# A gated linear recurrence with a SiLU feed-forward block on one core: a block of short products of several tile shapes behind the last product

## The chip, the cores and the metric

The kernel runs on one core of one Trainium2 chip. The metric is the device time of one execution in microseconds (us); of several executions the median is given. A profile of one execution lies beside the times. Its engines are called by the names of the profile: PE is TensorE's matmul, PEld its weight load, DVE VectorE, ACT ScalarE, POOL GpSimd and SP SyncE; a name with a q behind it (PEldq, SPq) is that engine's instruction queue, where waits, branches and transfers are issued.

## What is computed

Two blocks follow each other. The first is a recurrence over 768 steps for 4 batches of 8 heads with 48 x 48 complex states; the second takes its output as 3072 tokens of 384 numbers through a feed-forward block with 2048 hidden units.

```python
for t in range(S):                                   # S = 768, per batch and head, D = 48
    S_re, S_im = a_re*S_re - a_im*S_im + outer(k[t], v[t]),  a_re*S_im + a_im*S_re
    y[t] = q[t] @ S_re                               # a normalised to a magnitude of at most 0.999
x = y.transpose(0, 2, 1, 3).reshape(3072, 384)
h = x @ w_in                                         # 384 x 2048
out = (h * sigmoid(h)) @ w_out                       # 2048 x 384
```

## The kernel before

The 3072 tokens are cut into 24 chunks of 128 steps (`n`), two chunks make a pair (`p`, 12 of them). For each chunk the recurrence becomes products of 128 x 128 weights with the running state of 96 rows (48 real, 48 imaginary): `state` and `state_of_pairs` (lines 695 to 719) sum keys and values into the new state, `weights` (line 607) makes the scores, `output` (line 629) the result. For each pair the feed-forward block runs in eight steps `jp`: `hidden` makes two times 128 hidden units in one PSUM bank of the tag `h` (two banks that take turns, pool `p_h`, line 138), `silu` evicts it on ACT, and `result` adds its product with the second weight matrix into four (or two) accumulators `o`.

From pair 2 on the products of the feed-forward block are done in three parts of a shorter float type (`fp32r`), so that the sum has nearly the precision of float32. One set of parts, the rounded second weight matrix `W["coarse"]` (line 900, 128 rows x 16 x 384), stays in SBUF until the end. It is written by ACT (line 904) in the first third of the span and only read from then on.

The products of the recurrence are plain float32. On PE each of them is two records of weights and two of products, as the counts show: line 705 stands for 6 chunks x 8 heads, that is 48 products, and has 96 records. A `fp32r` product is one record.

The shapes matter below. Line 705 multiplies weights of 128 rows x 96 columns with 48 moving columns and uses the whole array. Lines 645, 648 and 716 write to `ps[64 * r:64 * r + 64]` with r = 0 and 1 in turn, so each uses one half of the array's columns. No product of the kernel before uses 64 rows, half of the array's rows, alone.

The order of all work is written out by hand in one long string of steps (lines 1129 to 1271), which is issued under `manual_schedule`; each engine gets its instructions in that order. Its last steps are `r:11.7` (the last twelve products, line 1004), then `oc:11.0` and `oc:11.1` (line 1014), which evict the last two accumulators, each in two halves, one on DVE (line 1021) and one on ACT (line 1023), and store them (line 1034). Behind the string every engine reads the flag `weak` (`values_load`, line 1279) and branches on it (line 1280) past a slower second program that is not taken here. Then the program closes: SP waits for one semaphore after the other, and all engines meet (the lines 1280 and 1442 of the profile).

Of the kernel before, what the change touches and what calls it, by code (L numbers as in the profile page):

```python
# [11 lines left out]
F32 = mybir.dt.float32  # L12
# [58 lines left out]
def kernel(  # L71
# [19 lines left out]
    nc = tc.nc  # L91
    B, H, S, D = q.shape
    C = 128
# [4 lines left out]
    D2 = 2 * D  # L98
# [4 lines left out]
    T = 2 * C  # L103
# [34 lines left out]
    p_h = Ring(fast.enter_context(tc.tile_pool(name="p_h", bufs=1, space=PSUM)), 2)  # L138
# [307 lines left out]
    def upper(n, x):  # L446

        p, i = divmod(n, 2)
        t = X[n][x] = room("left").tile([C, 2, DM], F32R, tag="part", name=f"{x}_parts{n}", bufs=1)
        nc.scalar.copy(out=t[:, 0], in_=cut(A[p][x], i))  # L450

    def lower(n, x):

        p, i = divmod(n, 2)
        t = X[n][x]
        nc.vector.tensor_tensor(out=t[:, 1], in0=cut(A[p][x], i), in1=t[:, 0].bitcast(F32),
                                op=ALU.subtract)
# [74 lines left out]
    def decayed(n, which="kq"):  # L532
        x = X[n]
        for w in which:
            e, at = x["e" + w], x[w].rearrange("p h d -> p (h d)")
            to = at if n < STRAIGHT else e
            if w == "k" and n >= STRAIGHT:
                nc.vector.scalar_tensor_tensor(out=to, in0=e, scalar=MOST, in1=at, op0=ALU.min,
                                               op1=ALU.mult)
            else:  # L540
                nc.vector.tensor_tensor(out=to, in0=at, in1=e, op=ALU.mult)
            x["e" + w] = to
            x[w, "decayed"] = True

    def rotated(n, which="kq", hs=slice(None)):

        x = X[n]
        for w in which:
            e = x["e" + w]
            if w + "r" not in x:  # L550
                spare = w == "k" and n in (1, 3)
                if spare:
                    x[w + "r"] = spare_form("xH", n // 2, f"{w}r{n}").rearrange(
                        "p (h c d) -> p h c d", h=H, c=2)
                else:
                    x[w + "r"] = att.tile([C, H, 2, D], F32, tag=w + "r", name=f"{w}r{n}", bufs=1)
            to, cs = x[w + "r"][:, hs], x["cs"][:, hs]
            nc.vector.tensor_tensor(
                out=to, in0=heads(e)[:, hs].unsqueeze(2).to_broadcast(list(to.shape)), in1=cs,
                op=ALU.mult)  # L560
# [26 lines left out]
    def squared(n, i):  # L587
        x = X[n]
        if "sq" not in x:
            x["sq"] = room("left").tile([C, NB, 2, HH, 2 * Q], F32, tag="sq", name=f"sq{n}", bufs=1)  # L590
        to = x["sq"][:, :, i].rearrange("p b h (j r) -> p b h r j" if i == 0 else
                                        "p b h (r j) -> p b h r j", r=2)
        of = x["kq"[i] + "r"].rearrange("p h c d -> p h (c d)")
        nc.vector.transpose(to, of.rearrange("p (h r) (b j) -> p b h r j", r=2, j=Q))
# [225 lines left out]
    V = {}  # L820
# [75 lines left out]
    W = {}  # L896
# [139 lines left out]
    def warm(n):  # L1036
# [3 lines left out]
        for _ in range(n):  # L1040
            nc.tensor.matmul(ps[:, 0], lhsT=any_[:, 0:C], rhs=any_, start=True, stop=True)

    def half_of(n, w, i):
        rotated(n, w, slice(i * HH, (i + 1) * HH))

# [50 lines left out]
    for name, f in {  # L1096
            "e0": early_square, "e1": early_magnitude, "e2": early_log, "e3": early_half,
            "e4": early_excess, "e5": early_l, "e6": early_add, "e7": early_inverse,
            "e8": early_ratio, "exp": decays, "phase": phases, "rd": rounded, "turn": turn,
            "trig": trig,  # L1100
            "ends": ends_of, "thirds": thirds, "L": summed, "carried": carried,
            "last": last_of, "dk": lambda n: decayed(n, "k"),
            "dq": lambda n: decayed(n, "q"), "K": lambda n: rotated(n, "k"),
            "Q": lambda n: rotated(n, "q"), "tk": lambda n: squared(n, 0),
            "tq": lambda n: squared(n, 1), "td": homed, "s": state, "ss": state_squared,
            "sd": state_homed, "S": carried_on, "y": output, "x": put, "xd": third_of,
            "ht": lambda n: upper(n, "th"), "hl": lambda n: upper(n, "l"),
            "ut": lambda n: lower(n, "th"), "ul": lambda n: lower(n, "l"),
            "xh": x_head, "xt": x_tail, "xg": x_diff,
            "vh": v_head, "vt": v_tail, "vk": v_kept, "vl": v_home,  # L1110
            "G0": squares, "G1": gates_log, "G2": gates_excess, "G3": gates_inverse,
            "G4": gates_l, "G5": magnitude, "G6": gates_ratio, "G7": gates_add,
            "G8": gates_side, "G9": gates_atan, "Ga": gates_angle, "of": finish,
            "wq": w_rounded, "wd": w_tail, "ws": w_diff, "wk": w_kept,
            "sm": small, "lk": looked_at, "ck0": check_decays, "ck1": check_low, "ck2": check_fit,
            "ck3": check_gathered, "ck4": check_weak,
    }.items():
        early[name] = lambda x, f=f: f(int(x))
    for name, f in {
            "rk": lambda n, i: half_of(n, "k", i), "rq": lambda n, i: half_of(n, "q", i),  # L1120
            "t": turned, "T": placed, "w": weights, "m": masked, "h": hidden, "g": silu,
            "lv": v_loaded, "vx": v_mixed, "oc": copied,
            "r": result, "gr": g_rounded, "gb": g_tail, "gc": g_diff,
            "lw": w_loaded, "at": lambda p, i: gates_atan(p, i),
            "an": lambda p, i: gates_angle(p, i),
    }.items():
        early[name] = lambda x, f=f: f(*map(int, x.split(".")))
    with tc.manual_schedule():
        for x in """
# [137 lines left out]
                r:11.4 lw:10.6 h:11.7 gc:11.5 lk:30 r:11.5 g:10.6 gr:10.6 h:10.7 gb:10.6 gc:10.6  # L1267
                lw:10.7 g:11.7 gb:11.6 lk:29 gc:11.6 r:10.6 gr:11.7 g:10.7 gr:10.7 ck2:0 gb:11.7
                gb:10.7 gc:10.7 ck3:0 r:10.7 ck4:0 oc:10.0 r:11.6 gc:11.7 oc:10.1 r:11.7 oc:11.0
                oc:11.1  # L1270
                """.split():
            what, _, arg = x.partition(":")
            early[what](arg)
# [173 lines left out]
```

## Time and profile before

| | |
|---|---|
| median of 2 executions | 606.19 us (605.37 to 607.02) |
| profiled execution, span from its first to its last instruction | 603.4 us |
| what lies around the span, by the median | 2.8 us (2.0 to 3.6 by the two executions) |
| PE, PEld busy | 583.3 us (97%), 509.3 us (84%) |
| DVE, ACT, POOL busy | 495.7 us (82%), 441.2 us (73%), 222.5 us (37%) |
| granted TensorE clock, mean of the span | 0.984 |

The profile gives no time of its own for the profiled execution besides its span; the median stands 2.8 us above it. A row of the timeline gives a start and a length in us from the first instruction, then engine, line, operation, output<-inputs with weights x moving operand, and a count. A record's length is longer than the time to the next record's start, because products are pipelined: where the price of a product is wanted, starts are compared. The granted clock is 1.00 at the higher of TensorE's two levels (2.4 GHz) and 0.50 at the lower (1.2 GHz).

### The profile page before, as it was taken

The page shows a single profiled execution, that of the slowest core. Times are in us where ns is not written, and L with a number is a line of the kernel's source. Part 1 is how long each engine was busy: PE and PEld are TensorE (multiplying, and loading weights), DVE is VectorE, ACT ScalarE, POOL GpSimd, SP SyncE. Part 2 cuts the span into 40 slices and gives each one's busy share as a digit, 9 for nine tenths or more (in the row PEclk, how much of TensorE's full clock was granted, in tenths as well). Part 3 has the DMA queues.
Part 4 walks back from the last instruction along what each step waited for, and adds up shares of the span by engine and source line. Part 5 has one row for each costly group of instructions (what it writes and reads, how often), then busy time and mean ns, then how long its engine had stood idle before and what let it go on. Part 6 is the DMA issues. An engine that isn't in the chain of part 4 may idle for free. (4 is left out here: it accounts for less than half of the span.)

```text
span 603.4 us, 11507 instructions
## 1 busy us (share of the span) xinstructions
PE 583.3 (97%) x3828; PEld 509.3 (84%) x3828; DVE 495.7 (82%) x765; ACT 441.2 (73%) x695; POOL 222.5 (37%) x389
## 2 busy tenths in 40 slices
PE   8588999999999999999999999999999999999997
PEld 6367877787767998998898898998898898999996
DVE  5899999987998989989889888889878786654644
ACT  7999999889885698896898895897884552342332
POOL 6364543636231534554444441536720323000000
PEclk9589999999999999999999999999999999999999
DMA  8988688977869977777868777859768467445652
GB/s 177 253 186 197 181 195 185 224 195 174 224 206 265 216 187 185 161 152 209 193 162 210 162 158 204 174 147 211 151 169 245 141 183 205 147 155 172 210 184 83
DMA packets 167728, 112.23 MB, mean 186 GB/s; under 512 B 137724, under 2 KB 143424, under 8 KB 167664
## 3 DMA queue, kind: packets, MB, share of 16 engines
q1 hardware_dynamic: 151920, 89.69, 57.2%
q0 software_dynamic: 12288, 17.23, 14.4%
q10 hardware_dynamic: 3456, 4.52, 2.1%
q8 instruction: 32, 0.52, 0.4%
q14 instruction: 32, 0.26, 0.2%
HBM read 81.14 MB, written 11.47 MB: 153 GB/s over the span
## 5 line engine op out<-in xcount | busy, mean ns | idle before, releaser
L307 ACT ACT_TABLE_LOAD x69 | 88.5, 1283 | 2.3 <-ACT ot L1017 0.8
L313 ACT ACTIVATE g<-h 128x512 f32<-128x512 f32 x96 | 56.0, 593 | 46.0 <-PE h L783 23.9
L600 POOL DMA_DIRECT2D T<-sq x120 | 70.1, 609 | 31.1 <-PE a L613 10.6
L944 ACT ACTIVATE head<-g 128x512 fp32r<-128x512 f32 x75 | 47.2, 630 | 46.2 <-PE o L986 25.9
L888 DVE SCALAR_TENSOR_TENSOR tail<-g,head 128x512 fp32r<-128x512 f32 x75 | 51.3, 683 | 32.1 <-ACT head L944 16.7
L528 POOL DMA_DIRECT2D dec<-ends x48 | 32.7, 722 | 117.6 <-DMA ends<-eq 116.8
L986 PE MATMUL o<-coarse,head 128*128 128x384 f32 x256 | 57.1, 344 | 0.5 <-ACT ot L1017 0.5
L766 PE MATMUL h<-xL,fine 128*128 128x512 f32 x192 | 55.3, 396 | 0.4 <-DMA fine<-w_firsts 0.4
L766 PE MATMUL h<-xD,mixed 128*128 128x512 f32 x192 | 55.2, 396 | 0.4 <-DVE xD L892 0.3
L986 PE MATMUL o<-diff,gd 128*128 128x384 f32 x256 | 55.4, 337 | 0.0
L892 DVE TENSOR_TENSOR gd<-tail,g 128x512 fp32r<-128x512 f32 x75 | 51.5, 687 | 4.3
L734 POOL DMA_DIRECT2D S<-ssq x84 | 46.8, 601 | 16.2 <-DVE ssq L723 10.3
L613 PEld LDWEIGHTS a<-T 96*128 96x128 f32 x384 | 49.9, 196 | 2.6 <-ACT T L605 0.3
L613 PE MATMUL a<-T 96*128 96x128 f32 x384 | 51.7, 281 | 0.1
L986 PEld LDWEIGHTS o<-coarse,head 128*128 128x128 f32 x256 | 44.8, 188 | 4.1 <-issue 1.1
L986 PE MATMUL o<-fine,tail 128*128 128x384 f32 x224 | 48.0, 336 | 0.0
L986 PEld LDWEIGHTS o<-diff,gd 128*128 128x128 f32 x256 | 45.5, 188 | 0.2 <-DVE gd L892 0.2
L776 PE MATMUL h<-xT,w 128*128 128x256 f32 x192 | 43.7, 381 | 1.6 <-ACT xT L689 1.6
L766 PEld LDWEIGHTS h<-xD,mixed 128*128 128x128 f32 x192 | 35.7, 188 | 10.1 <-DVE xD L892 1.2
L766 PEld LDWEIGHTS h<-xL,fine 128*128 128x128 f32 x192 | 36.0, 188 | 9.4 <-DMA fine<-w_firsts 0.8
L968 PE MATMUL o<-w,g 128*128 128x384 f32 x128 | 43.5, 488 | 0.0
L776 PEld LDWEIGHTS h<-xT,w 128*128 128x128 f32 x192 | 36.0, 190 | 7.9 <-ACT xT L689 1.8
(182 smaller groups left out, 1400.1 us busy)
## 6 DMA issues: line engine op xcount, KB each, us to landing
fine<-w_firsts SPq DMA_DIRECT2D x40, 384.0 KB
diff<-w_diffs SPq DMA_DIRECT2D x40, 384.0 KB
T<-sq SPq DMA_DIRECT2D x120, 64.0 KB
T<-sq POOLq DMA_DIRECT2D x120, 64.0 KB, 3.6
small<-in_moe_w_in_dram SPq DMA_DIRECT2D x16, 384.0 KB
raw<-in_moe_w_out_dram SPq DMA_DIRECT2D x16, 384.0 KB
small<-in_moe_w_out_dram SPq DMA_DIRECT2D x16, 384.0 KB
raw<-in_moe_w_in_dram SPq DMA_DIRECT2D x24, 192.0 KB
```

The lines of the kernel that those rows point to most:

```text
L307: nc.scalar.preload_act_table_set(SETS[of][0])
L313: nc.scalar.activation(out=out, in_=in_, func=func, **kw)
L600: (nc.gpsimd if a % 2 else nc.sync).dma_start(out=to[ts(b, Q), :, a], in_=X[n]["sq"][ts(a, Q), b].rearrange("p w h x -> p (w h) x"))
L613: nc.tensor.matmul(ps[:, h], lhsT=x["kT"][hh * HH + h], rhs=x["qT"][hh * HH + h], start=True, stop=True)
L734: (nc.gpsimd if g % 2 else nc.sync).dma_start(out=to[ts(b, Q), r, :, e], in_=sq[ts(g, Q), :, b, 0:e.stop - e.start])
L766: nc.tensor.matmul(ps, lhsT=w[:, dc, ts(p % 2, C)], rhs=x[:, :, dc], start=(f == 0 and dc == 0), stop=(f == len(forms) - 1 and dc == ND - 1))
L776: nc.tensor.matmul(ps[:, ji], lhsT=of_first(w1, dc, jp * 2 + ji), rhs=A[p]["xT"][:, dc], start=(dc == 0), stop=(dc == ND - 1))
L888: nc.vector.scalar_tensor_tensor(out=dst, in0=whole, scalar=MORE / FINER, in1=head.bitcast(F32), op0=ALU.mult, op1=ALU.subtract)
L892: nc.vector.tensor_tensor(out=dst, in0=tail, in1=whole, op=ALU.subtract)
L944: nc.scalar.mul(g_form(p, jp, "head"), A[p]["g", jp], MORE * SPLIT / FINER)
L968: nc.tensor.matmul(A[p]["o"][m].rearrange("p n c -> p (n c)"), lhsT=A[p]["g", jp][:, ji, ts(m, C)], rhs=w2[jp][:, ji], start=(j == 0), sto ...
L986: nc.tensor.matmul(A[q_]["o"][m].rearrange("p n c -> p (n c)"), lhsT=left[:, i, ts(m, C)], rhs=right, start=(first_ and n == 0), stop=(las ...
```

## The change

A step `after` is added, and put behind the last step of the order. It issues 100 products on PE, all from `W["coarse"]`, into tiles of the two banks of the tag `h`, which no one reads. `plain` is the same memory called float32, so 88 of the 100 are float32 products (two records each) and the 12 with 384 moving columns are `fp32r` (one record). In order: three groups of 16 with 64 rows, upper and lower half of the rows in turn, into two banks (96, 128 and 96 weight columns, 48, 48 and 64 moving columns); 8 over all rows, 96 x 48; 8 with 64 rows, 128 x 384; 8 with 96 rows and 64 columns, the halves of the columns in turn; 16 with 64 rows and 64 columns, the four quarters of the array in turn; 8 with 64 rows, 96 x 48; 4 over all rows, 128 x 384. Nothing else changes; the output is the same.

```diff
+    def after(_):
+        of = W["coarse"].rearrange("p j n -> p (j n)")
+        plain = of.bitcast(F32)
+        other = V["coarse", 4]
+
+        def bank():
+            return p_h.tile([C, 2, T], F32, tag="h", name="after").rearrange("p i x -> p (i x)")
...
+        for wide, narrow in ((D2, D), (C, D), (D2, 64)):
+            two = [bank(), bank()]
+            for i in range(8):
+                for s in range(2):
+                    at = slice(64 * s, 64 * s + 64)
+                    nc.tensor.matmul(two[s][0:wide, ds(narrow * (i % 8), narrow)],
+                                     lhsT=plain[at, ds(128 * i, wide)],
+                                     rhs=plain[at, ds(2048 + 64 * i, narrow)], start=True, stop=True)
+        one = bank()
+        for i in range(8):
+            nc.tensor.matmul(one[0:D2, ts(i, D)], lhsT=plain[:, ds(128 * i, D2)],
+                             rhs=plain[:, ds(2048 + 64 * i, D)], start=True, stop=True)
+        two = [bank(), bank()]
+        for i in range(4):
+            for s in range(2):
+                at = slice(64 * s, 64 * s + 64)
+                nc.tensor.matmul(two[s][:, 0:384], lhsT=of[at, ts(i, C)],
+                                 rhs=of[at, 2048:2432], start=(i == 0), stop=(i == 3))
+        two = [bank(), bank()]
+        for i in range(4):
+            for r in range(2):
+                nc.tensor.matmul(two[0][64 * r:64 * r + 64, ts(i, 64)], lhsT=plain[0:D2, ts(r, 64)],
+                                 rhs=plain[0:D2, 0:64], start=True, stop=True)
+        for i in range(4):
+            for s in range(2):
+                for r in range(2):
+                    at = slice(64 * s, 64 * s + 64)
+                    nc.tensor.matmul(two[s][64 * r:64 * r + 64, ds(256 + 64 * i, 64)],
+                                     lhsT=plain[at, ts(2 * i + r, 64)],
+                                     rhs=plain[at, ds(2048 + 64 * i, 64)], start=True, stop=True)
+        two = [bank(), bank()]
+        for i in range(4):
+            for s in range(2):
+                at = slice(64 * s, 64 * s + 64)
+                nc.tensor.matmul(two[s][0:D2, ts(i, D)], lhsT=plain[at, ds(128 * i, D2)],
+                                 rhs=plain[at, ds(2048 + 64 * i, D)], start=True, stop=True)
+        ps = bank()
+        for i in range(4):
+            nc.tensor.matmul(ps[:, 0:384], lhsT=of[:, ts(i, C)], rhs=of[:, 2048:2432],
+                             start=(i == 0), stop=(i == 3))
...
-                oc:11.1
+                oc:11.1 after:0
```

On PE, at the end of the program of before, the flag's load and the branch follow the last product of pair 11 (`o_1` is its second accumulator):

```order
L1004 MATMUL o_1_6293<-coarse,forms_7_6748 128x384 x2
L1004 MATMUL o_1_6293<-fine_1828,forms_7_6748 128x384 x2
L1004 MATMUL o_1_6293<-diff_7_6729,forms_7_6748 128x384 x2
L1279 TENSOR_LOAD weak [waits DVE_49]
L1280 COMPARE_AND_BRANCH
```

The same place now. Here 96x48 is the output of one product (weight columns x moving columns), x16 a count, and PE_49 the semaphore that PE itself raises, so such a wait is PE's for its own earlier product in that bank:

```order
L1004 MATMUL o_1_6293<-diff_7_6729,forms_7_6748 128x384 x2
L1061 MATMUL after<-coarse 96x48 [waits PE_49] x2
L1061 MATMUL after<-coarse 96x48 x14
L1061 MATMUL after<-coarse 128x48 [waits PE_49] x2
L1061 MATMUL after<-coarse 128x48 x14
L1061 MATMUL after<-coarse 96x64 [waits PE_49] x2
L1061 MATMUL after<-coarse 96x64 x14
L1066 MATMUL after<-coarse 96x48 [waits PE_49]
L1066 MATMUL after<-coarse 96x48 x7
L1072 MATMUL after<-coarse 128x384 [waits PE_49] x2
L1072 MATMUL after<-coarse 128x384 x6
L1077 MATMUL after<-coarse 64x64 [waits PE_49]
```

It goes on in the same way to the branch:

```order
L1077 MATMUL after<-coarse 64x64 x7
L1083 MATMUL after<-coarse 64x64 x2
L1083 MATMUL after<-coarse 64x64 [waits PE_49]
L1083 MATMUL after<-coarse 64x64 x13
L1090 MATMUL after<-coarse 96x48 [waits PE_49] x2
L1090 MATMUL after<-coarse 96x48 x6
L1094 MATMUL after<-coarse 128x384 [waits PE_49]
L1094 MATMUL after<-coarse 128x384 x3
L1333 TENSOR_LOAD weak [waits DVE_49]
L1334 COMPARE_AND_BRANCH
```

All 100 products stand between the last product that is used and PE's load of the flag. On the other engines no instruction moved against another.

## Rows read from the trace of the kernel before

**Rows 1.** The page: span, busy time and instructions of each engine, granted clock in 40 slices.
```profile
span 603.4 us, 11507 instructions
...
PE 583.3 (97%) x3828; PEld 509.3 (84%) x3828; DVE 495.7 (82%) x765; ACT 441.2 (73%) x695; POOL 222.5 (37%) x389
...
PEclk9589999999999999999999999999999999999999
```
**Rows 2.** Timeline of all engines behind 598.5 us: start, length, engine, line, what.
```profile
598.57 0.34 PE L1004 MATMUL o<-diff,forms 128*128 128x384 f32 x1
...
599.00 0.36 DVE L1021 COPY ot<-o 128x192 f32<-128x192 f32 x1 [0.70 <-PEq L1280]
...
599.39 0.32 ACT L1023 COPY ot_1b<-o 128x192 f32<-128x192 f32 x1 [0.74 <-DVE ot L1021]
599.74 0.34 ACTq L1034 DMA_DIRECT2D out_dram<-ot_1b  x1
```
**Rows 3.** Windows of the tail: stretch, its length, busy times, granted clock, DMA share, GB/s.
```profile
600.50:601.00 0.50, 0.00 (x0) 0.00 (x0) 0.00 (x0) 0.00 (x0) 0.00 (x0) 1.00 0.80 252
601.00:601.50 0.50, 0.00 (x0) 0.00 (x0) 0.00 (x0) 0.00 (x0) 0.00 (x0) 1.00 0.06 16
601.50:602.00 0.50, 0.00 (x0) 0.00 (x0) 0.00 (x0) 0.00 (x0) 0.00 (x0) 0.54 0.06 16
602.00:602.50 0.50, 0.00 (x0) 0.00 (x0) 0.00 (x0) 0.00 (x0) 0.00 (x0) 0.50 0.00 0
```
**Rows 4.** Queue instructions of lines 1280 and 1442: durations ns, first and last start us.
```profile
L1280 PEldq EVENT_SEMAPHORE  x1: 51/51/51, 599.0 to 599.0; - x1
...
L1442 SPq EVENT_SEMAPHORE  x14: 17/28/28, 601.7 to 603.3; - x14
...
L1442 PEldq EVENT_SEMAPHORE  x2: 51/51/51, 602.7 to 603.3; - x2
```
**Rows 5.** Timeline of PE, whole-array fp32r products with 384 moving columns.
```profile
597.69 0.52 PE L1004 MATMUL o<-coarse,forms 128*128 128x384 f32 x2
598.04 0.51 PE L1004 MATMUL o<-fine,forms 128*128 128x384 f32 x2
```
**Rows 6.** Timeline of PE, float32 products 96 x 48 on the whole array.
```profile
65.25 1.48 PE L705 MATMUL s<-v,l 128*96 128x48 f32 x16
66.57 0.68 PE L613 MATMUL a<-T 96*128 96x128 f32 x4
```
**Rows 7.** Timeline of PE, float32 products with 128 weight and 128 moving columns.
```profile
47.05 1.06 PE L613 MATMUL a<-T 96*128 96x128 f32 x8
47.94 0.60 PE L582 MATMUL tp<-ident,qr 128*96 128x128 f32 x4
```
**Rows 8.** Timeline of PE, float32 products on 64-column halves, 96 moving columns.
```profile
135.49 0.88 PE L716 MATMUL s<-kr,v 128*64 128x96 f32 x16
136.30 0.38 PE L613 MATMUL a<-T 96*128 96x128 f32 x1
```
**Rows 9.** Timeline of PE, float32 products on 64-column halves, 128 moving columns.
```profile
231.82 0.44 PE L648 MATMUL y<-T,S 96*64 96x128 f32 x4
232.04 0.44 PE L645 MATMUL y<-w,v 128*64 128x128 f32 x4
232.26 0.44 PE L648 MATMUL y<-T,S 96*64 96x128 f32 x4
```
**Rows 10.** Line 705: duration of one record, min/median/max in ns.
```profile
L705 PE MATMUL s<-v,l x32: 206/248/249, 40.2 to 66.5; 128*96 128x48 f32 x32
```
**Rows 11.** PE's queue at lines 1279 and 1280: durations ns, start us.
```profile
L1279 PEldq TENSOR_LOAD <-weak x1: 687/687/687, 595.6 to 595.6; - x1
...
L1280 PEldq COMPARE_BRANCH  x1: 922/922/922, 596.4 to 596.4; - x1
```
**Rows 12.** Window of the stretch at the lower clock, columns as in rows 3.
```profile
17.86:34.93 17.07, 12.24 (x38) 7.30 (x36) 16.17 (x31) 16.65 (x26) 7.66 (x12) 0.50 0.87 236
```
**Rows 13.** PE's timeline ahead of and in that stretch.
```profile
17.54 0.73 PE L463 MATMUL phase<-th,upto_r 128*128 128x384 f32 x1 [2.76 <-DVE th L436]
...
24.96 1.51 PE L705 MATMUL s<-v,kr 128*96 128x48 f32 x8 [0.68 <-DVE kr L558]
26.28 1.61 PE L463 MATMUL phase<-th,upto_r 128*128 128x384 f32 x2
```
**Rows 14.** Groups by line and shape: products whose result nobody reads.
```profile
L1041 PE MATMUL idle<-upto_r 128*128 128x256 bf16 x84 | 12.2, 318 | 2.1 <-POOL upto_r L284 2.1
```

More of the change, by code (lines that the diff above doesn't have):

```diff
@@ L1041, in warm, with chain @@
             nc.tensor.matmul(ps[:, 0], lhsT=any_[:, 0:C], rhs=any_, start=True, stop=True)
+    def after(_):
[4 more added lines that the diff above has]
+            return p_h.tile([C, 2, T], F32, tag="h", name="after").rearrange("p i x -> p (i x)")
+        def chain(n, wide, left, right):
+            ps = bank()[:, 0:wide]
+            for i in range(n):
+                nc.tensor.matmul(ps, lhsT=left(i), rhs=right(i), start=(i == 0), stop=(i == n - 1))
+        for wide, narrow in ((D2, D), (C, D), (D2, 64)):
[38 more added lines that the diff above has]
+                             start=(i == 0), stop=(i == 3))
@@ L1115 @@
             "sm": small, "lk": looked_at, "ck0": check_decays, "ck1": check_low, "ck2": check_fit,
-            "ck3": check_gathered, "ck4": check_weak,
+            "after": after, "ck3": check_gathered, "ck4": check_weak,
     }.items():
```

## The prediction

> **What bounds the kernel now.** I read the page first: PE is busy for 583.3 of 603.4 us, at the higher clock but for a short stretch near the start [rows 1]. PE bounds the body, and the change doesn't touch the body: it only adds work behind PE's last product. So all of the answer lies in the last five microseconds and in the price of the added products. I read the timeline of the tail next. PE's last product starts at 598.57 us and ends at 598.91; the last halves of the accumulator are evicted by DVE from 599.00 and by ACT to 599.71, and the last store is issued at 599.74 [rows 2]. From there no engine works: the windows show the DMA engines at a share of 0.80 to 601.0, 0.06 behind, and nothing from 602.0 [rows 3]. The queue rows show the rest: PE passes its own closing wait at 599.0; SP makes fourteen short waits in a row from 601.7 to 603.3, and the second last meeting of all engines, PE among them, is at 602.7 [rows 4]. So the program ends by the last store and SP's closing walk, and PE stands idle meanwhile.
>
> That idle time is the cover. The walk asks for each engine's semaphore in turn, so PE has to be done somewhere between 601.7, where the walk starts, and 602.7, where the engines meet. PE's closing wait comes at 599.0, so the cover is 2.7 to 3.7 us. Which of the fourteen waits is PE's no row tells; I take 3.4, nearer to the later end, as the meeting is what PE must not be late for. What PE takes beyond that moves the end one for one.
>
> **The change part by part.** Nothing is removed or moved. Added are 100 products, 88 in float32 with two records each and 12 in fp32r with one: 188 records. Their operands lie in SBUF since the first third of the span, no transfer is added, and no engine reads the results, so DVE, ACT, SP and the stores run as before. That they are really executed the 84 unread products of line 1041 show, which all have records [rows 14].
>
> Prices, from start to start. A float32 product of 96 x 48 on the whole array: 16 records from 65.25 to 66.57 [rows 6], 1.32 us for 8 products, 0.165 each. With 128 weight columns I have only line 613, which also has 128 moving columns: 8 records from 47.05 to 47.94 [rows 7], 0.222 a product. An fp32r product with 384 moving columns: two from 597.69 to 598.04 [rows 5], 0.175 each. A product on one half of the columns, the halves in turn: 16 records from 135.49 to 136.30 [rows 8], 0.101.
>
> The trace has no product on 64 rows alone, so its price is bounded from both sides. The upper end is that of the whole array: half of the rows takes as long as all. The lower end is half of that, if the two halves of the rows work side by side. For the halves of the columns the trace shows just this: lines 645 and 648 take 0.22 us for four records with 128 moving columns [rows 9], 55 ns a record, where line 613 on the whole array takes 111 ns for the same 128 columns [rows 7]. I take the lower end, because the halves of the columns are the nearest rows; the added code also gives each half of the rows a bank of its own, so that neither has to wait for the other's.
>
> Group by group, in us, upper end then taken: 16 of 96 x 48, 2.64 and 1.32; 16 of 128 x 48, 3.55 and 1.78; 16 of 96 x 64, 2.64 and 1.32 (with its 64 moving columns nearer to 0.165 than to 0.222); 8 of 96 x 48 on the whole array, 1.32 both; 8 of 128 x 384, 1.40 and 0.70; 8 on column halves, 0.81 both; 16 on quarters, at the price of column halves 1.62, and 0.81 if the row halves overlap too; 8 of 96 x 48, 1.32 and 0.66; 4 of 128 x 384, 0.70 both. The sums are 16.0 and 9.4 us.
>
> To this come PE's waits for itself. A group that writes to a bank of the group before waits until the products there are done. The first group's wait is for products of line 783 that ended long before, and at the quarters the bank is free too, so seven places are left. A record of line 705 lasts 248 ns [rows 10], and what waited for PE's last product started 0.09 us behind its end [rows 2]: 0.34 us from the last start of one group to the first of the next, where 0.08 would pass anyway. That is 0.25 us a place, 1.8 us in all; between nothing (the queue hides it) and 3 us (0.43, as behind the last product of 384 columns). The shape changes at nearly the same places. In the one change of rows 8 the next shape starts at 136.30, 0.07 us ahead of the end of the products before, so a change costs less than a wait for the end and is covered by it. The Trainium skill, page "TensorEngine Tiling (Array Packing)", Key Properties, has it that a change of the tiling mode drains TensorE; by this page a change would cost those 0.07 us more, 0.5 us over seven, and the row does not agree in full.
>
> Behind the block stands PE's load of the flag and its branch, 0.69 and 0.92 us, which ran from 595.6 to 597.3 while PE still had products queued until 598.91 [rows 2, 11]. They lie beside the last groups again, if PE's queue is as far ahead then; if not, up to 0.5 us is bare. I take 0.
>
> The sum: 9.4 + 1.8 = 11.2 us of PE, less 3.4 of cover: 7.8 us. The profiled execution's span would go from 603.4 to 611.2; with the 2.8 us around it that the median has, 606.2 becomes 614.0, 1.3% more. A measurement of this kernel tells about 2% from no change, 12.1 us, so this is within it.
>
> **The rivals.** First, the one on the slower side: halves of the rows don't work side by side. Then the block takes 16.0 + 1.8 = 17.8 us, 14.4 behind the cover: 620.6 us, 2.4% more. It decides from a block of 15.5 us on (12.1 + 3.4). For it speaks that no row shows two row halves at once; against it rows 9 and the two banks.
>
> Second, TensorE's clock falls inside the block. The clock stood at 0.50 from 17.86 to 34.93 us [rows 12], and it fell after PE had waited 2.76 us for DVE and then done little [rows 13]; in that stretch line 705 took 1.32 us for 8 records [rows 13], twice its price at the full clock. The block is of short products and stops seven times. If the clock falls half way, the products take 14.1 us in place of 9.4, 12.5 us behind the cover: 618.7; if it falls at once, some 623. Against it: the stops are a tenth of that 2.76 us, and the same products of line 705 run at full price at 65 us among other short ones [rows 6]. The Trainium skill, page "TensorE: Matmul & The Clock Gate", section "A second HAM failure mode: psum-queue depth-cycling", tells of a kernel that cycles through PSUM banks and lets the clock swing between its two levels by the short idle times between groups, which is what this rival would be.
>
> Third, the block costs nothing, because the records overlap far more than I think or the end waits for less of PE than I read: 606.2.
>
> **How the numbers follow.** The forecast, side by side at the full clock, has a chance of 0.68 with a range of its own from 611.5 (quarters four abreast, few waits) to 617; row halves one after the other 0.14; the clock 0.15; nothing 0.03. Slower by over 2% are most of the second and third: 0.11 and 0.10, and 0.03 of the forecast's upper tail, 0.24 in all. No case makes it faster; 0.01 is left for what I don't see. Within 2% is the rest, 0.75. The range goes from 611.0 to 621.5: it takes in the row halves one after the other with the spread of the two executions (0.8 us), and leaves out the block at no cost and the clock that falls at once.
>
> **What would show each step.** In the profile after, PE's last product before the block should still start near 598.6 and ACT's last eviction end near 599.7. The block should run from about 598.8 to 610, its 64-row groups at 41 ns a record (82 if they don't overlap, 160 and more at the lower clock), with seven gaps of about a quarter of a microsecond, and the granted clock at 1.00 until behind it. SP's closing waits should end about one microsecond behind PE's closing wait. A block of over 15.5 us, or a granted clock of 0.50 in it, would make the forecast wrong on the slower side; SP done before PE, or a block under 7 us, on the other.

## The result and the profile after

The changed kernel takes 613.4 us (613.2 and 613.6 in two executions) against 606.2: a ratio of 1.0117 with a 95% interval from 1.0098 to 1.0136, so 6 to 8 us more. It is within the 2% that count as no change, and 0.6 us from the forecast of 614.0. A second series of six executions gave 1.0144 (1.0119 to 1.0168), with 614.8 us as its median; five of the six lie between 613.6 and 615.5, one at 618.8.

The page of the changed kernel, its span, PE's row and the granted clock, stands against [rows 1]:

```profile
span 611.8 us, 11883 instructions
...
PE 594.4 (97%) x4016; PEld 519.1 (85%) x4016; DVE 495.5 (81%) x765; ACT 441.1 (72%) x695; POOL 224.1 (37%) x389
...
PEclk9689999999999999999999999999999999999999
```

PE has 188 records more, 4016 against 3828, and is busy 11.1 us longer. DVE's and ACT's counts stand where they were. The clock is at the upper level to the end, as before.

The timeline of the changed kernel from the last used products on (start, length, engine, line, what) answers to [rows 2]:

```profile
599.19 0.52 PE L1004 MATMUL o<-diff,forms 128*128 128x384 f32 x2
...
599.64 5.26 PE L1061 MATMUL after<-coarse 64*96 64x48 f32 x96
...
600.54 0.34 ACTq L1034 DMA_DIRECT2D out_dram<-ot_1b  x1
...
604.92 1.56 PE L1066 MATMUL after<-coarse 128*96 128x48 f32 x16
...
606.40 1.09 PE L1072 MATMUL after<-coarse 64*128 64x384 f32 x8
...
607.43 0.69 PE L1077 MATMUL after<-coarse 96*64 96x64 f32 x16
...
608.04 0.69 PE L1083 MATMUL after<-coarse 64*64 64x64 f32 x32
...
608.79 0.94 PE L1090 MATMUL after<-coarse 64*96 64x48 f32 x16
...
609.72 0.97 PE L1094 MATMUL after<-coarse 128*128 128x384 f32 x4
```

The last used product ends at 599.71, the block's last at 610.69: 10.98 us. The last store is issued at 600.54, 0.83 us behind the last used product, just as in the kernel before (599.74 behind 598.91). In this profile the last used product ends 0.80 us later than in that of before; a second profile of before has 599.61, so that end varies between executions, and it is not counted to the change. What is compared from here on is therefore the tail: from the end of the last used product to the end of the span. It is 12.13 us here and 4.45 in the first profile of before, 7.7 us more.

Who ends the program is read from the queue instructions of the closing lines (1442 of before is 1496 here, 1280 is 1334): count, shortest/median/longest in ns, first and last start:

```profile
L1496 SPq EVENT_SEMAPHORE  x14: 17/28/7328, 602.5 to 611.8; - x14
...
L1496 PEldq EVENT_SEMAPHORE  x2: 51/51/51, 611.2 to 611.8; - x2
```
```profile
L1334 PEldq COMPARE_BRANCH  x1: 388/388/388, 610.3 to 610.3; - x1
L1334 PEldq EVENT_SEMAPHORE  x1: 51/51/51, 610.8 to 610.8; - x1
```

For whom SP waits there (for whom: us, times, longest):

```profile
SPq L1496 <- PEq L1333: 7.3, 1, 7.3
...
SPq L1496 <- PEq L1334: 0.4, 1, 0.4
```

SP starts its closing walk at 602.5 and stands 7.3 us in one of its fourteen waits, for PE's load of the flag, and 0.4 us in a later one, for PE's branch; all fourteen were 17 to 28 ns each in [rows 4]. PE's branch takes 0.39 us, and its closing wait comes at 610.77, 0.08 behind the last product. From there it is 1.07 us to the end. That is the whole of the change: the walk used to end on SP's own time, and now it waits for PE.

### The profile page after: what moved, and what is told of

The parts are those of the page before. It is cut to its first block, busy times and chain, and to the rows that moved or that the text cites. A ratio compares the mean times of both kernels' runs of the same rounds, so it can differ in the third digit from the quotient of the medians.

```text
span 611.8 us, 11883 instructions
## 1 busy us (share of the span) xinstructions
PE 594.4 (97%) x4016; PEld 519.1 (85%) x4016; DVE 495.5 (81%) x765; ACT 441.1 (72%) x695; POOL 224.1 (37%) x389
## 4 chain that ended last, share of the span: by engine, by line
PE 83%; ACT 9%; DMA 3%; DVE 3%; issue 2%; POOL 0%; ACTq 0%; SPq 0%; DVEq 0%; POOLq 0%
PE o L986 21%; PE h L766 20%; PE h L776 6%; PE h L783 6%; PE a L613 6%; PE o L1004 6%; PE o L968 4%; PE y L645 3%; PE y L648 3%; ACT L307 2%; PE idle L1041 2%; ACT s L313 2%; PE s L716 2%; DMA out_dram<-ot 1%; DMA w_diffs<-diff 1%
## 5 line engine op out<-in xcount | busy, mean ns | idle before, releaser
L600 POOL DMA_DIRECT2D T<-sq x120 | 70.1, 608 | 31.5 <-PE a L613 11.2
L766 PE MATMUL h<-xH,firsts 128*128 128x512 f32 x144 | 42.7, 405 | 0.0
```

The costliest lines, as they stand in the source:

```text
L600: (nc.gpsimd if a % 2 else nc.sync).dma_start(out=to[ts(b, Q), :, a], in_=X[n]["sq"][ts(a, Q), b].rearrange("p w h x -> p (w h) x"))
L766: nc.tensor.matmul(ps, lhsT=w[:, dc, ts(p % 2, C)], rhs=x[:, :, dc], start=(f == 0 and dc == 0), stop=(f == len(forms) - 1 and dc == ND - 1))
```

## The experiments

All of them compute the whole output; only the unread products differ. "Block" is the time from the end of the last used product to the end of the last unread one, "tail" that to the end of the span, both in the profiled execution.

**Is it the row halves?** Every product on 64 rows goes to rows 0 to 63 (at four places):

```
-                    at = slice(64 * s, 64 * s + 64)
+                    at = slice(0, 64)
```

> Every product of the block that lies on 64 rows is put on rows 0 to 63, where the changed kernel has every other one on rows 64 to 127; number, sizes and banks of the products stay. My theory: the low price in the block (two records about every 85 ns) comes from two row halves working beside each other. Then these groups double (1.32 to 2.6, 1.75 to 3.5, 1.37 to 2.7, and the smaller ones by 0.5 to 0.7 each), the block goes from 11.0 to 17 us, and the time to 619.4 us. Rival: the low price is that of short products as such, on whatever rows; the block stays at 11.0 us and the time at 613.4 us.

Measured: 628.8 us, a ratio of 1.0378 (1.0355 to 1.0401), 9 us above what the theory gave. The timeline of this kernel:

```profile
599.86 12.20 PE L1061 MATMUL after<-coarse 64*96 64x48 f32 x96
611.99 2.79 PE L1066 MATMUL after<-coarse 128*96 128x48 f32 x16
```

Windows of the same kernel (stretch, length, busy time and records of PE, PEld, DVE, ACT, POOL, granted clock, DMA share, GB/s):

```profile
599.40:601.40 2.00, 2.00 (x21) 1.75 (x21) 0.36 (x1) 0.59 (x2) 0.00 (x0) 1.00 0.36 119
...
605.40:607.40 2.00, 2.00 (x15) 2.00 (x14) 0.00 (x0) 0.00 (x0) 0.00 (x0) 0.59 0.00 0
607.40:609.40 2.00, 2.00 (x15) 2.00 (x14) 0.00 (x0) 0.00 (x0) 0.00 (x0) 0.50 0.00 0
```

Two causes lie on top of each other. In the first group, at the upper clock, one record starts every 85 ns, where the changed kernel starts two, 7 ns apart, every 85 ns. So it is the row halves: on one half the price is twice as high, as the theory had it. Then, 5.9 us into the block, the clock falls at 605.8 and stays low to the end. The group on the whole array, which this edit does not touch, goes from 1.56 us to 2.79. All four executions had a granted clock of 0.965 to 0.971 over the span, below the 0.981 to 0.990 of the kernel before on the same chip; only one of them has a trace. The block is 24.96 us long, 14 more than in the changed kernel. By the prices at the upper clock the row halves are about 6 of these 14, an estimate from the lengths of the 64-row groups in the changed kernel, and the clock about 8.

**What sets the price of a record?** Four groups with other sizes in place of the block:

```
-        for wide, narrow in ((D2, D), (C, D), (D2, 64)):
+        for wide, narrow in ((D2, 16), (D2, 96), (D2, 128), (64, 16)):
```

> The block is replaced by four groups of 16 fp32 products on alternate row halves, with 96 weight columns and 16, 96 and 128 moving columns, and with 64 weight columns and 16 moving columns. My theory: a pair of records on the two halves takes the time of the longer of its weight columns and its moving columns: a pair starts every 85, 85, 110 and 57 ns, so the groups take 1.4, 1.4, 1.8 and 0.9 us. Rival: the load of the weights alone sets it: 85, 85, 85 and 57 ns. Second rival: the moving columns count and 48 and 64 only chanced to agree: the first and last group would take under half of the second.

Measured: from first to last start 1.30, 1.39, 1.76 and 0.94 us; inside a group a pair starts every 85, 85, 109 and 58 ns. The theory holds: with 16, 48, 64 or 96 moving columns 96 weight columns cost the same, and 128 columns on either side cost 109 to 112. Both rivals fall, the first by the third group, the second by the first and the last.

This kernel took 612.8 us in its one execution, though its block is only 6.4 us long. Its tail is 9.73 us, of which 3.4 lie behind the last product (607.68 to 611.05), where the changed kernel has 1.15. The queue instructions of its line 1302 show why:

```profile
L1302 PEldq COMPARE_BRANCH  x1: 2407/2407/2407, 607.5 to 607.5; - x1
L1302 PEldq EVENT_SEMAPHORE  x1: 51/51/51, 610.0 to 610.0; - x1
```

And the DMA packets of this kernel between 606.90 and 609.95 us, one in all (queue: packets, MB, share of 16 engines):

```profile
q8 instruction: 1, 0.02, 1.9%
```

PE's branch took 2.41 us instead of 0.39, and beside it ran an instruction load of 16 KB, from 607.55 to 608.47. The branch ended 1.45 us behind that load. The Trainium skill, page "Runtime: NRT & Kernel Launch", section "Instruction fetch mechanics", says that a taken branch whose target is not among the loaded pages waits for a load of 16 KiB. The trace agrees, with 2.4 us for the branch, though it does not tell what the load holds. In the changed kernel the last load of this queue ahead of the branch was over at 607.25, 3.1 us before the branch began, and the branch took 0.39.

**What are the pauses between groups?** The groups take turns between two pairs of PSUM banks:

```
+            turn[0] += 1
...
+            if turn[0] % 2:
+                return p_h.tile([C, 2, T], F32, tag="h", name="after").rearrange("p i x -> p (i x)")
+            return p_m.tile([C, 2, T], F32, tag="m", name="after").rearrange("p i x -> p (i x)")
```

> The whole block, but its groups take turns between two pairs of PSUM banks, so that a group no longer opens a bank that the group straight ahead of it wrote. My theory: the pauses of 0.15 to 0.30 us between the groups of the changed kernel are the waits of PE for its own last results in the bank, and the change of tile shape costs nothing beside them. Then the pauses fall to some 0.05 us at every place, those with a change of shape among them, the block from the end of the last used product to its own last end goes from 11.0 to about 9.2 us, and the time to 611.7 us. Rival: a change of shape drains the array by itself. Then the two pauses between the first three groups, which have one shape, go, the other six stay near 0.2 us, and the block is 10.4 us. Second rival: the pause is neither, but the first product of a group waiting for its weights; nothing moves, 11.0 us.

Measured: the block is 9.99 us, 0.99 shorter, between what the theory (9.2) and the first rival (10.4) gave. The time is 612.2 us, 1.0108 (1.0081 to 1.0134), which does not tell it from the changed kernel. The weight loads of the changed kernel, with the idle time ahead of a row and who ended it:

```profile
601.25 3.51 PEld L1061 LDWEIGHTS after<-coarse 64*128 64x128 f32 x64 [0.17 <-PE after L1061]
604.91 1.44 PEld L1066 LDWEIGHTS after<-coarse 128*96 128x96 f32 x16 [0.15 <-PE after L1061]
...
607.42 0.55 PEld L1077 LDWEIGHTS after<-coarse 96*64 96x64 f32 x16 [0.25 <-PE after L1072]
...
608.79 0.81 PEld L1090 LDWEIGHTS after<-coarse 64*96 64x96 f32 x16 [0.19 <-PE after L1083]
```

The same rows with four banks:

```profile
599.43 4.58 PEld L1069 LDWEIGHTS after<-coarse 64*96 64x96 f32 x96 [0.26 <-issue]
604.08 1.43 PEld L1075 LDWEIGHTS after<-coarse 128*96 128x96 f32 x16
...
606.47 0.55 PEld L1088 LDWEIGHTS after<-coarse 96*64 96x64 f32 x16 [0.25 <-issue]
...
607.71 0.76 PEld L1102 LDWEIGHTS after<-coarse 64*96 64x96 f32 x16
```

With four banks the first three groups are one row of 96 loads without a pause: where the shape stays, the wait for the bank was all, 0.21 and 0.18 us from start to start beyond the usual step. At 604.08 the shape changes and no wait stands there: the step is 0.175 us, 0.09 beyond the usual 0.085. In the changed kernel, with wait and change at this place, it is 0.26, 0.175 beyond. So the two do not add up; the wait covers the change. Of six changes of shape without a wait, each costs 0.09 us at the step into the new shape, and 0.04 to 0.11 more at the second step in it. The Trainium skill, page "TensorEngine Tiling (Array Packing)", Key Properties, has a change of the tiling mode drain TensorE. The trace agrees in that each change costs a pause. But the new shape starts at 604.08, 0.07 us ahead of the recorded end of the products before it (604.15), so a wait for that end is not what it shows.

**Is the space behind the last product free?** First with two groups, the eight products 96x48 on the whole array and the four at the end (the rest of the block is deleted).

> Of the block only two groups stay, the eight 96x48 products on the whole array and the four fp32r products 384 wide at the end; 2.2 us in all. My theory: the first 3.4 us behind the last used product are free, since the store of the output and the closing walk of SP's queues run beside them. Then the time is that of the kernel before, 606.2 us, and the span from the last used product to the end is that of before within 0.2 us. Rival: nothing is free, each us of PE work behind the last product moves the end by one; 608.4 us.

Measured: 608.1 us, 1.0022 (1.0010 to 1.0035), 1.3 us more than before (0.6 to 2.1). That is neither free nor one for one. The block is 2.09 us, and PE's closing wait is at 603.42; SP's walk ends at 606.6. So PE is not what is late. SP's waits in this kernel (for whom: us, times, longest):

```profile
SPq L1302 <- SPq L1302: 3.2, 3, 2.2
```

and in the changed kernel:

```profile
SPq L1334 <- SPq L1334: 1.5, 3, 0.5
```

These waits are for the stores of the output; the view puts a wait for a landing down to SP's own line. From the issue of the last store to the wait that it releases it is 3.49 us here, 1.73 in the changed kernel and 1.71 in the profile of before. Then three groups, 48 products:

> Of the block only the first three groups stay, the 48 products on row halves; they end 5.3 us behind the last used product. My theory: 3.4 us of it lie under the cover, the other 1.9 us move the end one for one; 608.1 us. Rival, nothing is free: 611.5 us. Rival, the end is moved by the number of groups or instructions and not by when PE is through: with 96 of 188 records half of the change's cost, 609.8 us.

Measured: 608.2 us, 1.0028 (1.0016 to 1.0041), 1.7 us more, where the theory had 1.9. The block is 5.19 us, the store takes 1.74, and 1.11 us stand between the last product and the end; PE is what SP waits for last:

```profile
SPq L1302 <- SPq L1302: 1.5, 3, 0.6
SPq L1464 <- PEq L1301: 1.5, 1, 1.5
...
SPq L1464 <- PEq L1302: 0.4, 1, 0.4
```

So a block two and a half times as long costs nearly the same. To find out whether the short block makes the store late, or whether that was chance, it was run twice more, and the kernel before once more:

> The kernel with two groups only, once more with a profile: in the first the last store of the output landed 3.5 us behind its issue, in the kernel before 1.7 us. Theory A: that was chance; here it lands after 1.7 to 1.9 us and the span from the last used product to the end is 4.5 us as in the kernel before. Theory B: the two groups make it late; 3.5 us again, and 6.2 us from the last used product to the end.

> The same kernel a third time, as a further profile of the last store. Theory A, chance: 1.7 to 1.9 us from issue to landing and 4.5 us from the last used product to the end. Theory B, caused by the two groups: 3.5 us and 6.2 us.

> The kernel before, with a second profile. If the last store's landing varies by itself (theory A), this profile may show more than the 1.7 us of the first, and then 4.5 us between the last used product and the end are no fixed size either; if the two groups cause it (theory B), 1.7 to 1.9 us and 4.5 us again. The last used product ends at 598.9 us in the first profile; the changed kernels had 599.4 to 601.3, and I expect some 599.7 us here, since the median of the times lies 1 us above the profiled one.

Measured, from issue to landing: 3.63 and 3.52 us with the short block, tails of 6.38 and 6.26 us, the times 609.1 and 608.8. So it is the short block that makes it late (theory B), three times in three. But the kernel before had 3.21 us this time, and a tail of 5.95 instead of 4.45: there it varies by itself. SP's waits in this second profile of it:

```profile
SPq L1280 <- SPq L1280: 2.6, 5, 1.4
```

Neither theory is whole. The DMA queues of the short block's first profile, between 603.05 and 604.50 us:

```profile
q10 hardware_dynamic: 118, 0.08, 16.7%
q8 instruction: 1, 0.02, 5.9%
q14 instruction: 3, 0.02, 5.9%
```

and between 604.50 and 605.20:

```profile
q10 hardware_dynamic: 8, 0.01, 5.6%
```

Queue 10 carries the last store. All but nine of its packets are through at 603.43. Queue 8 loads 16 KB of instructions from 603.12 to 604.49, queue 14 two pages at 603.4 and one to 604.58, and the last nine packets follow one after the other up to 605.13, eight of them in the second window. Nine packets, eight of 768 bytes and one of 4, are a sixteenth of the 144 of this store: one DMA engine's share, if the 16 engines divide it evenly, which the trace does not tell. In the other two profiles of the short block the last packets go on at 604.31 and 603.92, the loads on queue 8 end at 604.32 and 603.95.

The load starts 0.7 us behind the end of PE's branch (602.40), as in the first profile of before (597.32, 598.03). In all fourteen profiles queue 8 has a load 0.7 to 1.2 us behind that end, and so it is taken for PE's. In the first profile of before the branch is early and the load over at 599.08, ahead of the last store's issue at 599.74. In the second the last 18 packets of the last two stores come from 602.26 to 603.03, behind a load on queue 14 that ended at 602.26. So far this is an argument from times. If it is right, a longer block must cost less, because it puts the branch and the load behind the store:

```
-        for wide, narrow in ((D2, D), (C, D), (D2, 64)):
+        for wide, narrow in ((D2, D),):
```

The eight products on the whole array stay, and what follows them is deleted.

> Of the block two groups stay, the first (16 products 96x48 on row halves) and the eight 96x48 on the whole array: 3.2 us behind the last used product, 1.1 us more than the short one of two groups. In that one PE's branch came 0.7 to 1.1 us behind the last used product, a 16 KB instruction load of PE followed 0.7 us later, and the last nine packets of the output's store stood behind it. My theory: here the branch and so the load come later than the store's packets; the store lands 1.7 to 1.9 us behind its issue, the span from the last used product to the end is 4.4 to 4.6 us against 6.2 to 6.4 there, and the time is below that of the shorter block, 606.6 us against 608.1. Rival: any block in which PE is still busy when the store is issued makes the store late: 3.5 us, 6.3 us to the end, 608.2 us or more.

Measured, in twelve executions: 606.7 us, a ratio of 0.9999 (0.9983 to 1.0015) with a block of 3.10 us. The shorter block of 2.09 us had 1.0022 (1.0010 to 1.0035). Each ratio is to the kernel before on the same chip; the two intervals overlap between 1.0010 and 1.0015. So 50% more work costs less, as the theory had it, if not by a wide margin, and the rival's 608.2 falls. Its waits, though:

```profile
SPq L1306 <- SPq L1306: 2.4, 3, 1.3
```

The store still took 2.66 us in the profiled execution, not 1.7 to 1.9, and the tail is 5.40 us, not 4.5. One packet of 4 bytes was left at 603.26, behind a load on queue 14 from 602.89 to 603.26; PE's load came at 604.60, out of the way. The large load was moved by this edit, and the nine late packets are gone with it. From that last packet to SP's wait it is another 1.01 us, against 0.4 to 0.6 in the other profiles; nothing in the trace tells what takes the rest. That queue 14's loads hold up what is left rests on their times alone.

**Does the clock fall?** The block twice in a row:

```
-                oc:11.1 after:0
+                oc:11.1 after:0 after:0
```

> The block stands twice behind the last used product. My theory: the second copy costs its own length, as the first beyond the cover, and the clock stays at its upper level; 11.0 + 11.2 - 3.4 = 18.8 us over the kernel before, 625.0 us, with the granted clock 1.00 until the block is through. Rival: so many short products in a row bring the clock down to its lower level after more than the 11 us of the first copy; the second copy then takes up to 22 us, 636 us, and the granted clock shows 0.50 within it.

Measured: 627.0, 627.6, 634.5 and 640.1 us; without the longest the ratio is 1.0390 (1.0328 to 1.0453). Two executions lie 2 us and more above the theory, one near the rival, one beyond it. The profiled one is the longest; its windows, with columns as above:

```profile
599.40:601.40 2.00, 1.95 (x40) 1.82 (x41) 0.36 (x1) 0.32 (x1) 0.00 (x0) 1.00 0.59 192
601.40:603.40 2.00, 1.99 (x37) 1.86 (x37) 0.00 (x0) 0.00 (x0) 0.00 (x0) 1.00 0.06 17
603.40:605.40 2.00, 2.00 (x29) 1.83 (x26) 0.00 (x0) 0.00 (x0) 0.00 (x0) 0.53 0.00 0
605.40:607.40 2.00, 2.00 (x14) 2.00 (x13) 0.00 (x0) 0.00 (x0) 0.00 (x0) 0.50 0.04 8
```

and the same stretches of the changed kernel:

```profile
599.40:601.40 2.00, 1.95 (x37) 1.59 (x35) 0.36 (x1) 0.38 (x2) 0.00 (x0) 1.00 0.45 147
601.40:603.40 2.00, 1.99 (x34) 1.86 (x35) 0.00 (x0) 0.00 (x0) 0.00 (x0) 1.00 0.19 62
603.40:605.40 2.00, 1.99 (x38) 1.85 (x38) 0.00 (x0) 0.00 (x0) 0.00 (x0) 1.00 0.00 0
```

The clock fell at 603.5, 4.1 us into the first copy, which is the changed kernel's own block, and stayed low to the end. Up to 603.5 the two have the same work, and PE is busy 1.95 and 1.99 of 2.00 us in both. So the second copy is not what brings the clock down; the rival as it was put falls too. What did bring it down here and not there no run shows. In this execution PE's branch took 3.80 us and its closing wait came 2.8 us behind the last product; if the branch is as long at the upper clock, that is the 2 us by which even 627.0 lies above the theory.

```profile
L1334 PEldq COMPARE_BRANCH  x1: 3802/3802/3802, 633.5 to 633.5; - x1
```

To see how often this strikes the changed kernel, it was run again:

> The changed kernel once more, in more executions. The doubled block was twice seen with the clock at its lower level from inside the first copy on, and the block moved ahead once in four. My theory: this strikes some executions of the changed kernel too, as an addition of up to 10 us (the 7 us of the block that are left, at half the clock, and more), while most stay at 612 to 614.5 us. Rival: the single block behind the last product is too short for it; no execution is above 615 us.

Measured: 613.6, 613.9, 614.5, 615.1 and 615.5 us with a granted clock of 0.983 to 0.989, and 618.8 with 0.976. The profiled execution (615.1) has a block of 10.98 us and a tail of 12.14, to 0.01 us those of the first; it is longer by a last used product that ends at 601.16, and so 615.1 speaks for neither side; 615.5, with a clock of 0.986, has no trace. The one at 618.8 has none either. Its granted clock and its time fit a fall inside the block, as the theory had it and as the rival in the prediction priced it (618.7), but that is not shown.

**The same block where PE is waited for.** It moves ahead of the last rotation but one step:

```
-                gb:10.7 gc:10.7 ck3:0 r:10.7 ck4:0 oc:10.0 r:11.6 gc:11.7 oc:10.1 r:11.7 oc:11.0
-                oc:11.1 after:0
+                gb:10.7 gc:10.7 ck3:0 r:10.7 ck4:0 oc:10.0 r:11.6 gc:11.7 oc:10.1 after:0 r:11.7 oc:11.0
+                oc:11.1
```

> The whole block stands ahead of the last rotation's products but one place, so that used products and the output's store follow it and PE's end is no longer beside the closing walk. My theory: the 3.4 us that were free behind the last product are free only there; here PE is what all else waits for, so the end moves by the whole block, 11.0 to 11.3 us, to 617.3 us. Rival: the block fills time in which PE waits anyway wherever it stands; 613.4 us or less.

Measured: 617.0, 617.2, 617.3 and once 623.5 us, 1.0219 (1.0165 to 1.0273); the theory had 617.3. The one at 623.5 had a granted clock of 0.973, where the others had 0.982 to 0.988, and has no trace. The timeline of this kernel around the block:

```profile
596.67 0.85 PE L1004 MATMUL o<-diff,forms 128*128 128x384 f32 x4
597.45 5.26 PE L1061 MATMUL after<-coarse 64*96 64x48 f32 x96
...
607.55 0.97 PE L1094 MATMUL after<-coarse 128*128 128x384 f32 x4
608.35 0.52 PE L1004 MATMUL o<-coarse,forms 128*128 128x384 f32 x2
```

The groups have the lengths of the changed kernel, and the used products go on at 608.35, where they would have at 597.36: 10.98 us in full. Behind the last product the tail is 4.65 us, as before. So the free part belongs to the place behind the last product, and not to the block.

## Why the prediction was right

- **PE bounds the body, the change sits behind it.** Held. The body's end varies by itself: the last used product ends at 598.91 and 599.61 us in the two profiles of before, at 599.71 and 601.16 in the two of the changed kernel. A difference of 7 us stands above that, one of 1.3 us only over many executions.
- **The cover of 3.4 us.** It held for the profile that it was read from: 10.98 us of block less 7.68 of longer tail is 3.30, and 1.1 us between PE's closing wait and the end is what the prediction had for SP's walk. The block of three groups gives 3.34, 5.19 us of block less 1.86 of longer tail (6.31 against 4.45). Which of the fourteen waits is PE's, which the prediction had to guess, the changed kernel shows: PE's branch ends the eleventh, which stood at 602.34 in the kernel before, 3.34 us behind PE's closing wait. But the cover was taken as a fixed size, and it is not one. The end of the kernel before is the landing of its last store, 1.71 or 3.21 us behind the issue, and with the latter the cover would be 4.8. The sentence "the program ends by the last store and SP's closing walk" was right; that the store's landing varies by 1.5 us no row of one profile could show.
- **The row halves side by side.** Held, and shown by the edit to one half: two records every 85 ns on two halves, one on one. The first three groups were put at 1.32, 1.78 and 1.32 us and took 1.32, 1.75 and 1.37 from their first start to their last.
- **The column halves and the quarters.** Both too dear at 0.81 us: 0.46 and 0.48. They were priced by rows with 96 moving columns at 64 weight columns [rows 8]; the sizes here are 64 and 64, and the longer of the two counts, as the run with other sizes shows.
- **The waits, seven at 0.25 us.** The sum came out, its make-up did not. With the usual steps taken away, 2.0 us of pauses are left against 1.8 predicted: of 10.71 us from the block's first start to its last, 8.69 are steps of 58 to 175 ns. With four banks 1.0 of this is gone; the other half are changes of shape and the first pair of a group. That the wait covers the change was right where both stand. So the block's 11.2 us against 10.98 is in part luck: the products were priced 0.5 us too dear in sum, the pauses 0.2 too cheap.
- **The 2.8 us around the span.** Not a fixed size. In the result and in every later execution 1.7 to 1.9 us lie between the span and the time (611.8 and 613.6 in the profiled one); the rest of the 2.8 was that the median of before stood above the profiled execution.
- **The load of the flag and the branch, at no cost.** Right here by luck of place: 0.04 us more than before between the last product and PE's closing wait. Two of the other blocks had a branch of 2.4 and 3.8 us, and PE was 2.3 and 2.8 us late by it. The prediction's upper bound of 0.5 us for this term was too low.
- **The rivals.** Row halves one after the other: refuted, and the time forecast for it (620.6) would have been too low against 628.8, since in the run that made them so the clock fell as well. The clock: it stayed up in the profiled execution of the result and, by the mean granted clock, in the other one and in five of six later, and may have fallen in the sixth, which has no trace. A chance of 0.15 does not stand against that. No cost: refuted for the whole block, true for one of 3.1 us.

## What to carry to other kernels

Behind PE's last used product there is free time as long as the landing of the last store and the closing walk last longer. Beyond that each microsecond counts in full: from three groups to the whole block PE works 5.79 us longer, and the tail grows by 5.83. Ahead of the last used product there was none. Look at the store's landing in more than one profile before you call the free time a number. On tiles of 64 rows count pairs, not products: a float32 pair on the two halves costs what the longer of its weight and moving columns costs, 58 ns at 64, 85 at 96 and 109 to 112 at 128.

## What was not expected

- A block of 2.1 us behind the last product cost 1.3 us, one of 3.1 us nothing that could be told from the kernel before. With the shorter one an instruction load of 16 KB, 0.7 us behind PE's branch, met the packets of the last store, and the store landed 3.5 to 3.6 us behind its issue in place of 1.7. That the load is the cause rests on the times and on the longer block.
- PE's branch at the end took 0.39 to 0.48 us in most of these kernels, 0.92 and 1.36 in the kernel before, 2.4 and 3.8 in two blocks. In these four it ended 1.4 to 1.5 us behind the end of a 16 KB instruction load.
- The granted clock can fall from 1.00 to 0.50 while PE is busy without a break, 4.1 us into a block of short products, and not fall in another execution of the same products. In the kernel with one row half it fell in the profiled execution and, by the mean granted clock, in the other three. What decides it stays open.
